# A banded convolution on TensorE quadrants: lag of the upper rows, order of the first pair of batches, and place of the transforms

## The chip, the cores and the metric

The kernel runs on one core of a Trainium2 chip. A core has a matrix engine (TensorE, "PE" in the profile, with "PEld" for its weight loads), VectorE ("DVE"), ScalarE ("ACT"), GpSimd ("POOL", which here also issues most of the DMAs) and SyncE ("SP"). The engines run side by side. Each takes its own instructions in the order of the program and waits on semaphores for the others. The metric is the device time of one execution in microseconds (us).

## The reference

The input `x` has shape (8, 3264, 192): batch, sequence, channels. Two layers follow each other.

The first is a causal convolution along the sequence. Each of 8 heads (24 channels each) has 7 taps, a softmax over `weight`:

```
w = softmax(weight, axis=-1)
u[b,s,c] = sum_k w[h(c),k] * x[b, s-6+k, c]        (zeros before s = 0)
```

The second mixes the lowest 64 frequencies and then a dense layer:

```
X = rfft(u, axis=1)[:, :64]
Y = X[b,m,:] @ (w_r[m] + i*w_i[m])                 (64 complex 192x192 matrices)
v = u + irfft(Y)
out = v + max(v @ w_ch, 0)
```

## The kernel before

The batches go in four pairs `q` (2 batches each). A sequence of 3264 is cut into 13 blocks of 256. A block lies in SBUF as 128 partitions by two rows: partition `p` holds positions 2p and 2p+1 of the block, and the choice between the two is called `a`. So a pair has 26 tiles of 128 rows (`NT`), and all of `x` in bf16 is the tile `xall`.

The convolution runs in units of blocks. Pair 0 has units of 3, 5 and 5 blocks, each later pair a unit of 7 and one of 6: nine units, with indices k = 0 to 8. A unit has 16 steps: 8 heads, and for each the output rows a = 0 and a = 1. A step is a product of a banded 64x64 matrix (tile `shared`, called `band`) with `n` blocks of one head (48n columns; 336 for n = 7, 288 for 6, 240 for 5, 144 for 3). TensorE is split into four 64x64 quadrants. A step has four matmuls on the lower 64 rows and four on the upper 64 rows, and all eight add into one PSUM bank (`conv_pieces`, matmuls at L299). Two row halves must not write one bank at the same time, so `conv_step` (L305) runs the lower rows of step k together with the upper rows of step k-2, and before them puts a `turn`: a wait of TensorE's queue until the lower rows of step k-2 have ended. Each step takes the next bank of a ring of seven (`conv_bank`, L284). `xtrans` takes two banks of the same ring.

A bank is emptied by a copy that casts to bf16 and writes back into `xall`: VectorE for a = 0 (L326), ScalarE for a = 1 (L328). The output of a unit goes one block lower than its input stood, in the slots that the halo of both steps of a head still reads. So the two copies of a head are emitted after the upper rows of its a = 1 step, and both wait for those.

Between the steps stand other works, in an order written out by hand in the loop at L378:

- `dft` (L330, matmuls at L334): the product of a finished tile of `xall` with 128 columns of cosines and sines (`ftab`), 26 tiles added up per pair in one bank of its own, which `xs` (L337) copies out. `dfts` issues them in groups: 3 and 3 in the second unit, 5 and 5 in the next two, up to 7 and 7 later, at heads 3 and 7 (5 and 7 in the second unit).
- `xtrans` (L339): 12 small matmuls that turn the frequencies of a pair for the mixing, with one copy on VectorE (L355) and one on ScalarE (L357); at head 1 of units 4, 6 and 8.
- `table` (L220): the cosine and sine table, in three parts of tiles and six operations each, three on VectorE (L224, L227, L229) and three on ScalarE (L231, L233, L235), spread by `extra` over the heads of the first three units.

Ahead of the loop VectorE computes the softmax and sets the taps in a packed band (seven `copy_predicated` for each half of the heads, L205). Four copies of 32 partitions for each half then put it in place, two on VectorE (L215) and two on ScalarE (L213). A dummy sine (L191) makes ScalarE load its sine table early. It writes `wrec`, which the reciprocal of the softmax (L195) writes next. TensorE meanwhile runs `NIDLE` = 28 matmuls on zeros.

GpSimd issues the loads of `x` (`load_unit`, L144), each casting from f32 in HBM. Between them it builds constants: `ident`, `perm`, `apart`, and parts of `wm` and `w1`. Then come the loads of the mixing matrices.

After the convolution follow the mixing by frequency (L458) among transposes (L419), from 80 to 119 us, and the inverse transform with the dense layer (L667, copies at L570 and L583), from 119 us to the end. The change does not touch them.

Of the kernel before, what the change touches and what calls it, by code (L numbers as in the profile page):

```python
# [10 lines left out]
ACT = mybir.ActivationFunctionType  # L11
AX = mybir.AxisListType
F32 = mybir.dt.float32
# [6 lines left out]
def kernel(  # L20
# [9 lines left out]
    nc = tc.nc  # L30
    B, S, D = x.shape
    H, KK = weight.shape
# [4 lines left out]
    P = 128  # L37
# [6 lines left out]
    BW = P + 2  # L44
    TWOPI = 6.283185
    MAGIC = 12582912.0
    NIDLE = 28
    UNITS0 = ((0, 3), (3, 5), (8, 5))
    UNITS = ((0, 7), (7, 6))
    units = [(q, b0, n) for q in range(NQ) for b0, n in (UNITS if q else UNITS0)]  # L50
# [3 lines left out]
    def sb(name, shape, dtype):  # L54
        return pool.tile([P] + shape, dtype, tag=name, name=name)
# [14 lines left out]
    band = shared[:, 0:H * 2 * BW].rearrange("p (h o c) -> p h o c", h=H, o=2)  # L70
# [7 lines left out]
    ascale = sb("ascale", [1], F32)  # L78
# [21 lines left out]
    def temp(n, dtype):  # L100
        w = n * 2 if dtype == F32 else n
        a = arena[:, pos[0]:pos[0] + w]
        pos[0] += (w + 15) // 16 * 16
        return a.bitcast(dtype) if dtype != BF16 else a
# [8 lines left out]
    wmax = temp(H, F32)  # L113
    wsum = temp(H, F32)
    wrec = temp(H, F32)
    cidx = temp(PW, F32)
    goff = temp(1, F32)
    masks = temp((KK // 2 + 1) * PW, U16)
# [25 lines left out]
    def load_unit(q, b0, n):  # L144
        nf = min(n, NB - 1 - b0)
        s0 = NB * q + b0 + 1
        for i in range(2):
            off = ((2 * q + i) * S + 2 * P * b0) * D
            src = bass.AP(tensor=x.tensor, offset=x.offset + off, ap=[[2 * D, P], [2 * P * D, nf], [1, 2 * D]])
            nc.gpsimd.dma_start(out=xin[:, s0:s0 + nf, 2 * D * i:2 * D * (i + 1)], in_=src)  # L150
        if nf < n:
            off = (2 * q * S + 2 * P * (NB - 1)) * D
            src = bass.AP(tensor=x.tensor, offset=x.offset + off, ap=[[2 * D, PL], [S * D, 2], [1, 2 * D]])
            nc.gpsimd.dma_start(out=xin[0:PL, s0 + nf, :].rearrange("p (i c) -> p i c", i=2), in_=src)
# [24 lines left out]
    zeros = xall[:, 0, 0, 0:P]  # L179
    for _ in range(NIDLE):  # L180
        nc.tensor.matmul(ZC[6], zeros, zeros.unsqueeze(1).to_broadcast([P, 4, P]), start=True, stop=True,
                         skip_group_check=True)
# [5 lines left out]
    nc.vector.tensor_tensor(out=wsub.rearrange("p (h k) -> p h k", h=H), in0=wr3,  # L188
                            in1=wmax.unsqueeze(2).to_broadcast([P, H, KK]), op=ALU.subtract)
    nc.scalar.activation(out=wexp, in_=wsub, func=ACT.Exp)  # L190
    nc.scalar.activation(out=wrec, in_=ascale.to_broadcast([P, H]), func=ACT.Sin)  # L191
    we3 = wexp.rearrange("p (h k) -> p h k", h=H)
    nc.vector.reduce_sum(out=wsum, in_=we3, axis=AX.X)
    nc.vector.tensor_scalar(out=wsum, in0=wsum, scalar1=1e-9, scalar2=None, op0=ALU.add)
# [6 lines left out]
    for h0 in (0, H // 2):  # L201
        hs = slice(h0, h0 + H // 2)
        for lag in range(KK):
            k = lag // 2
            nc.vector.copy_predicated(  # L205
                out=pk4[:, hs, lag % 2, :],
                mask=masks[:, PW * k:PW * (k + 1)].unsqueeze(1).to_broadcast([P, H // 2, PW]),
                data=ta3[:, hs, KK - 1 - lag:KK - lag].to_broadcast([P, H // 2, PW]))
        for g in range(4):
            c0 = 1 + 32 * (g % 2)  # L210
            dst, srcv = band[32 * g:32 * g + 32, hs, :, c0:c0 + PW], pk4[32 * g:32 * g + 32, hs, :, :]
            if g % 2:
                nc.scalar.copy(out=dst, in_=srcv)  # L213
            else:
                nc.vector.tensor_copy(out=dst, in_=srcv)  # L215
# [4 lines left out]
    def table(step, t0, t1):  # L220
# [13 lines left out]
        else:  # L234
            nc.scalar.activation(out=ftab[:, t0:t1, 0:2 * MODES - 1:2], in_=wh, func=ACT.Sin, scale=-TWOPI,  # L235
                                 bias=halfpi[:, 0:1])

    nc.gpsimd.memset(ident[:], 0.0)
    nc.gpsimd.affine_select(out=ident[:], in_=ident[:], compare_op=ALU.not_equal, fill=1.0,
                            base=0, pattern=[[-1, P]], channel_multiplier=1)  # L240
# [2 lines left out]
                            base=-64, pattern=[[-1, 64]], channel_multiplier=1)  # L243
    nc.gpsimd.affine_select(out=perm[:, 64:128], in_=perm[:, 64:128], compare_op=ALU.not_equal, fill=1.0,
                            base=0, pattern=[[-1, 64]], channel_multiplier=1)
    load_unit(*units[3])

    for i in range(2):
        nc.gpsimd.memset(apart[i][:], 0.0)
        for c in range(2):  # L250
# [6 lines left out]
                            fill=1.0, base=0, pattern=[[-1, D]], channel_multiplier=1)  # L257
    nc.gpsimd.affine_select(out=w1[64:P, D:2 * D], in_=w1[64:P, D:2 * D], compare_op=ALU.not_equal,
                            fill=1.0, base=P, pattern=[[-1, D]], channel_multiplier=1)
    for k, u in enumerate(units[4:]):  # L260
        load_unit(*u)
        if k == 1:
            nc.gpsimd.dma_start(out=wm[:, 0:D], in_=moe_w_ch[0:P, :])
        if k == 2:
            nc.gpsimd.dma_start(out=w1[64:P, 0:D], in_=moe_w_ch[P:D, :])
# [11 lines left out]
    def turn(names):  # L277
        nop = nc.tensor.nop()
        for name in names:
            tc.add_manual_dep(nop.ins, name, mybir.DependencyInfo(mybir.DependencyClass.Sync,  # L280
                                                                  mybir.DependencyReason.DATA),
                              reason="row tiles take turns on a bank")

    def conv_bank():  # L284
        npass[0] += 1
        return ZC[(npass[0] - 1) % 7]
# [14 lines left out]
                                       tile_position=(64 * row, 64 * col), skip_group_check=True).ins.name  # L301

    flow = []

    def conv_step(u):  # L305

        lower = upper = iter(())
        flow.append(None)
        if u is not None:
            flow[-1] = [(u, conv_bank()), []]  # L310
            lower = conv_pieces(flow[-1][0], 0)
        old = flow[-3] if len(flow) > 2 else None
        if old is not None:
            turn(old[1][2:])
            upper = conv_pieces(old[0], 1)
        for _ in range(4):
            if u is not None:
                flow[-1][1].append(next(lower))
            next(upper, None)
        if old is not None and old[0][0][4] == 1:  # L320
            for (q, b0, n, h, a), z in (flow[-4][0], old[0]):
                s0 = NT * q + 2 * b0 + a
                dst = xall[:, s0:s0 + 2 * n - 1:2, :, GRP * h:GRP * h + GRP]
                srcv = z[:, 0:2 * GRP * n].rearrange("p (b i e) -> p b i e", b=n, i=2)
                if a == 0:
                    nc.vector.tensor_copy(out=dst, in_=srcv)  # L326
                else:
                    nc.scalar.copy(out=dst, in_=srcv)  # L328

    def dft(q, t0, t1):  # L330
        xp = zf
# [7 lines left out]
    def xtrans(q, banks=None):  # L339
        if banks is None:  # L340
            banks = [conv_bank(), conv_bank()]
        for i in range(2):
            tp = banks[i][:, 0:3 * P].rearrange("p (j c) -> p j c", j=3)
            xsv = xs[q % 2][:, i, :].rearrange("k (p j) -> k j p", j=3)
            for j in range(3):
                nc.tensor.matmul(tp[0:64, j, :], xsv[:, j, :], apart[0][:], start=True, stop=True,  # L346
                                 tile_position=(0, 0), skip_group_check=True)
                nc.tensor.matmul(tp[64:P, j, :], xsv[:, j, :], apart[1][:], start=True, stop=True,
                                 tile_position=(0, 64), skip_group_check=True)
        for i in range(2):  # L350
            b = 2 * q + i
            dst = xt[:, :, b:2 * B:B, 0:MODES]
            srcv = banks[i][:, 0:3 * P].rearrange("p (j c m) -> p j c m", j=3, c=2)
            if i == 0:
                nc.vector.tensor_copy(out=dst, in_=srcv)  # L355
            else:
                nc.scalar.copy(out=dst, in_=srcv)  # L357

    p1, p2, p3 = (0, 6), (6, 16), (16, NT)
    extra = {(0, 1): ((0, *p1),), (0, 2): ((1, *p1),), (0, 3): ((2, *p1),), (0, 4): ((3, *p1),), (0, 5): ((4, *p1),),  # L360
             (0, 6): ((5, *p1), (0, *p2)), (1, 0): ((1, *p2),), (1, 2): ((2, *p2),), (1, 3): ((3, *p2),),
             (1, 4): ((0, *p3),), (1, 5): ((4, *p2),), (1, 6): ((1, *p3),), (1, 7): ((5, *p2),),
             (2, 0): ((2, *p3),), (2, 2): ((3, *p3),), (2, 4): ((4, *p3),), (2, 6): ((5, *p3),)}
    todo = []
    pend = []

    def dfts(n):
        while n > 0 and todo:
            q, t0, t1 = todo.pop(0)
            m = min(n, t1 - t0)  # L370
            dft(q, t0, t0 + m)
            n -= m
            if t0 + m < t1:
                todo.insert(0, (q, t0 + m, t1))
            elif t1 == NT:
                pend.append(q)

    for k, u in enumerate(units):  # L378
        for h in range(H):
            for a in range(2):  # L380
                conv_step((*u, h, a))
            for e in extra.get((k, h), ()):
                table(*e)
            if h == 1 and pend:
                xtrans(pend.pop(0))
            if k == 1 and h in (5, 7):
                dfts(3)
            elif k > 1 and h in (3, 7):
                dfts(5 if k < 4 else 7)
        if k == 3:  # L390
            for g in range(NW + 3):
                load_w(g)
        todo.append((u[0], 2 * u[1], 2 * (u[1] + u[2])))
    for _ in range(2):
        conv_step(None)
    dfts(99)
    nc.gpsimd.memset(yet[:, :, 2 * B * (MODES - 8):2 * B * MODES], 0.0)
    zt4 = open_psum("left", (1, 1, 1, 1))
# [357 lines left out]
```

## Time and profile before

| | |
|---|---|
| median of three runs | 184.71 us (184.31 to 184.81) |
| the profiled execution's own time | 184.13 us |
| its span, first to last instruction | 182.3 us |
| TensorE busy | 167.5 us, 92% of the span |
| VectorE busy | 129.2 us, 71% |
| ScalarE busy | 113.8 us, 62% |
| GpSimd busy | 52.2 us, 29% |
| chain that ended last | TensorE 83%, VectorE 9%, ScalarE 3% |
| copies of the convolution on VectorE (L326) | 72 of 448 ns in the mean |
| copies of the convolution on ScalarE (L328) | 72 of 388 ns in the mean |
| transform matmuls (L334) | 104 of 327 ns |

The span leaves out 1.8 us of the execution's own time. A line of the timeline gives the start in us, the time in us, the engine, the line of the kernel, the operation, out<-in, the number of instructions that the line merges, and in brackets how long the engine had been idle and what ended that. Two forms of a group differ in shape, so a mean over a whole line mixes units of different size. A matmul's time reaches from its start to the end of its pipeline, so matmuls overlap.

### The profile page before, as it was taken

Reading aid. Unit: us, or ns where it says so; the run is one execution under the profiler, and the core shown is the slowest. Engines: PE = TensorE matmul, PEld = TensorE weight load, DVE = VectorE, ACT = ScalarE, POOL = GpSimd, SP = SyncE. Lnnn points to the kernel's source line nnn. Section 1 sums busy time; section 2 is a strip of 40 time slices with the busy share of each in tenths; the row PEclk is TensorE's granted clock in tenths of the full one; section 3 lists DMA queues with packets and bytes.
Section 4 is the critical chain, followed back from the end, with each engine's and each line's share of the span. In section 5 each row is a group of like instructions: output and inputs, shape, how many; then the busy total and the mean of one; then the engine's idle time right before and its main releaser. Section 6 shows DMA issues by size and latency. Waiting matters only on the chain.

```text
span 182.3 us, 7178 instructions
## 1 busy us (share of the span) xinstructions
PE 167.5 (92%) x2970; PEld 123.9 (68%) x2970; DVE 129.2 (71%) x278; ACT 113.8 (62%) x239; POOL 52.2 (29%) x95
## 2 busy tenths in 40 slices
PE   6949999999999999879999998899999999999990
PEld 2437554555555565458999946479989999999960
DVE  6698865555555464346877813679899999999992
ACT  5356866554564364238777724468888888888870
POOL 7997332334224442026503400088000000000000
PEclk9996999999999999999999999999999999999999
DMA  3999999999999999929995992058999898989996
GB/s 48 149 198 203 207 201 203 205 206 199 204 204 207 206 207 206 201 51 160 198 207 94 162 191 39 0 168 305 351 323 347 319 363 316 366 332 341 351 343 229
DMA packets 37392, 40.15 MB, mean 220 GB/s; under 512 B 2512, under 2 KB 37360, under 8 KB 37360
## 3 DMA queue, kind: packets, MB, share of 16 engines
q0 software_dynamic: 22848, 19.62, 68.4%
q1 hardware_dynamic: 14512, 20.09, 30.1%
q8 instruction: 23, 0.38, 0.8%
q14 instruction: 9, 0.07, 0.1%
HBM read 39.10 MB, written 20.05 MB: 324 GB/s over the span
## 4 chain that ended last, share of the span: by engine, by line
PE 83%; DVE 9%; ACT 3%; issue 2%; DVEq 0%; ACTq 0%
PE z L667 32%; PE z L299 21%; PE z L419 11%; PE z L334 10%; PE z L458 3%; DVE xall L326 2%; DVE arena L205 2%; PE z L537 1%; PE z L346 1%; PE z L594 1%; PE z L605 1%; PE z L528 1%; DVE xall L175 1%; PE z L538 1%; ACT L191 1%
## 5 line engine op out<-in xcount | busy, mean ns | idle before, releaser
L570 DVE TENSOR_TENSOR arena<-z,xall 128x384 f32<-128x384 f32 (+1 forms) x104 | 57.0, 556 | 3.3 <-PE z L667 1.3
L583 ACT ACTIVATE z<-z 128x384 f32<-128x384 f32 x102 | 48.5, 475 | 12.1 <-PE z L667 2.4
L326 DVE CAST xall<-z 128x336 bf16<-128x336 f32 (+3 forms) x72 | 32.0, 448 | 25.5 <-PE z L299 22.3
L299 PE MATMUL z<-xall,shared 64*64 64x288 bf16 (+3 forms) x1152 | 44.1, 290 | 4.9 <-DVE xall L326 3.8
L667 PE MATMUL z<-arena,ftab 64*128 64x384 bf16 x308 | 44.9, 322 | 0.0
L667 PEld LDWEIGHTS <-ct 64*128 64x128 bf16 x600 | 42.3, 94 | 3.7 <-PE z L594 0.6
L328 ACT CAST xall<-z 128x336 bf16<-128x336 f32 (+3 forms) x72 | 27.6, 388 | 24.5 <-PE z L299 21.3
L299 PEld LDWEIGHTS <-shared 64*64 64x64 bf16 x1152 | 27.4, 108 | 21.5 <-issue 9.4
L667 PE MATMUL z<-wsw,ct 64*128 64x192 bf16 x300 | 35.1, 243 | 0.0
L667 PEld LDWEIGHTS <-ftab 64*128 64x128 bf16 x396 | 29.7, 93 | 2.7 <-issue 0.5
L667 PE MATMUL z<-wm,ct 64*128 64x192 bf16 x200 | 29.9, 243 | 0.0
L667 PE MATMUL z<-w,ct 64*128 64x192 bf16 x100 | 24.3, 243 | 0.0
L411 DVE COPY ct<-z 128x1024 bf16<-128x1024 bf16 x26 | 17.1, 687 | 5.1 <-PE z L419 3.6
L334 PE MATMUL z<-xall,ftab 128*128 128x384 bf16 (+1 forms) x104 | 19.8, 327 | 0.6 <-DVE xall L326 0.6
L419 PE MATMUL z<-ident,xall 128*128 128x128 bf16 x312 | 19.3, 219 | 0.2 <-ACT ftab L409 0.2
L150 POOL DMA_DIRECT2D xall<-in_x_dram x18 | 15.8, 879 | 12.3 <-DMA xall<-in_x_dram 11.4
L419 PEld LDWEIGHTS <-xall 128*128 128x128 bf16 x312 | 17.7, 98 | 1.0 <-issue 0.3
L272 POOL DMA_DIRECT2D arena<-in_moe_w_r_dram x13 | 8.1, 622 | 32.0 <-PE z L458 24.2
L409 ACT COPY ct<-z 128x1024 bf16<-128x1024 bf16 x13 | 13.2, 1012 | 4.2 <-PE z L419 4.0
L334 PEld LDWEIGHTS <-ftab 128*128 128x128 bf16 (+1 forms) x104 | 8.9, 98 | 9.0 <-issue 4.5
L667 PE MATMUL z<-mixa,ftab 64*128 64x384 bf16 x88 | 13.6, 323 | 0.0
L485 POOL DMA_DIRECT2D arena<-xs x16 | 7.9, 504 | 14.7 <-ACT xs L481 14.6
(108 smaller groups left out, 135.7 us busy)
## 6 DMA issues: line engine op xcount, KB each, us to landing
out_dram<-arena SPq DMA_DIRECT2D x47, 384.0 KB, 3.5
xall<-in_x_dram POOLq DMA_DIRECT2D x6, 672.0 KB, 16.1
xall<-in_x_dram POOLq DMA_DIRECT2D x8, 480.0 KB, 15.7
arena<-in_moe_w_r_dram POOLq DMA_DIRECT2D x13, 288.0 KB, 8.2
arena<-in_moe_w_i_dram POOLq DMA_DIRECT2D x13, 288.0 KB, 9.0
ct<-in_moe_w_r_dram POOLq DMA_DIRECT2D x3, 288.0 KB, 11.7
ct<-in_moe_w_i_dram POOLq DMA_DIRECT2D x3, 288.0 KB, 11.7
out_dram<-arena SPq DMA_DIRECT2D x3, 288.0 KB, 3.0
```

Source lines behind the costliest of these rows:

```text
L150: nc.gpsimd.dma_start(out=xin[:, s0:s0 + nf, 2 * D * i:2 * D * (i + 1)], in_=src)
L272: nc.gpsimd.dma_start(out=wts[g][64 * half:64 * half + 64, :, :, :], in_=src[4 * g:4 * g + 4, :, :].rearrange("m (p j) e -> p m j e", j=3))
L299: yield nc.tensor.matmul(o, band[r, h, int(a != a1), c0:c0 + 64], xin5[r, s1:s1 + n, :, a1, dsl], start=(row == 0 and a1 == 0), stop=(row ...
L326: nc.vector.tensor_copy(out=dst, in_=srcv)
L328: nc.scalar.copy(out=dst, in_=srcv)
L334: nc.tensor.matmul(xp, ftab[0:k, t, :], xall[0:k, NT * q + t, :, :], start=(t == 0), stop=(t == NT - 1), skip_group_check=True)
L409: nc.scalar.copy(out=out, in_=in_)
L411: nc.vector.tensor_copy(out=out, in_=in_)
L419: nc.tensor.matmul(o, in_, ident[:], start=True, stop=True, is_transpose=True)
L570: nc.vector.tensor_tensor(out=o[0:pn, :, a, :], in0=bank[0:pn, 0:2 * D].rearrange("p (i d) -> p i d", i=2), in1=xall[0:pn, s + a, :, :], o ...
L583: nc.scalar.activation(out=z, in_=z, func=ACT.Relu)
L667: mm = nc.tensor.matmul(target(bank[k], cols, r), l, r, start=first, stop=last, skip_group_check=True)
```

## The change

- The upper rows run three steps behind the lower ones instead of two (`CONVLAG` = 3). `conv_step` takes the old step and the pair to copy one place further back.
- The copies of the two rows change engines: a = 0 goes to ScalarE, a = 1 to VectorE.
- Pair 0 runs unit by unit: after each of its three units a new `flush` issues the upper rows that are still open (three calls without a new step) and empties the list. Then come all transforms of that unit, and after the third unit also `xtrans` of pair 0. After the first unit's flush, six matmuls of 512 columns on the band run ahead of the transforms.
- From unit 4 on the transforms come once per unit, all 12 or 14 tiles at head 2, after the `xtrans` if one is open. In unit 3 there are none.
- The table's operations have other places in the first three units: up to three at one head.
- All four band copies of the first half of the heads are on ScalarE, all four of the second half on VectorE.
- The dummy sine writes a tile of its own, `wsin`.
- `NIDLE` is 27. The loads of units 3 and 4 are issued ahead of the constants on GpSimd; the loads of `wm` and `w1` come one unit later.

```diff
-    NIDLE = 28
+    NIDLE = 27
...
-    nc.scalar.activation(out=wrec, in_=ascale.to_broadcast([P, H]), func=ACT.Sin)
+    nc.scalar.activation(out=wsin, in_=ascale.to_broadcast([P, H]), func=ACT.Sin)
...
-            if g % 2:
+            if h0 == 0:
                 nc.scalar.copy(out=dst, in_=srcv)
             else:
                 nc.vector.tensor_copy(out=dst, in_=srcv)
...
+    load_unit(*units[3])
+    load_unit(*units[4])
     nc.gpsimd.memset(ident[:], 0.0)
...
-    load_unit(*units[3])
...
-    for k, u in enumerate(units[4:]):
+    for k, u in enumerate(units[5:]):
...
+    CONVLAG = 3
...
-        old = flow[-3] if len(flow) > 2 else None
+        old = flow[-1 - CONVLAG] if len(flow) > CONVLAG else None
...
-            for (q, b0, n, h, a), z in (flow[-4][0], old[0]):
+            for (q, b0, n, h, a), z in (flow[-2 - CONVLAG][0], old[0]):
...
                 if a == 0:
+                    nc.scalar.copy(out=dst, in_=srcv)
+                else:
                     nc.vector.tensor_copy(out=dst, in_=srcv)
-                else:
-                    nc.scalar.copy(out=dst, in_=srcv)
+
+    def flush():
+        for _ in range(CONVLAG):
+            conv_step(None)
+        flow.clear()
...
-    extra = {(0, 1): ((0, *p1),), (0, 2): ((1, *p1),), (0, 3): ((2, *p1),), (0, 4): ((3, *p1),), (0, 5): ((4, *p1),),
-             (0, 6): ((5, *p1), (0, *p2)), (1, 0): ((1, *p2),), (1, 2): ((2, *p2),), (1, 3): ((3, *p2),),
-             (1, 4): ((0, *p3),), (1, 5): ((4, *p2),), (1, 6): ((1, *p3),), (1, 7): ((5, *p2),),
-             (2, 0): ((2, *p3),), (2, 2): ((3, *p3),), (2, 4): ((4, *p3),), (2, 6): ((5, *p3),)}
+    extra = {(0, 0): ((0, *p1), (1, *p1), (2, *p1)), (0, 3): ((3, *p1), (4, *p1)), (0, 5): ((5, *p1),),
+             (0, 7): ((0, *p2), (1, *p2), (2, *p2)), (1, 1): ((3, *p2),), (1, 2): ((4, *p2), (0, *p3)),
+             (1, 3): ((5, *p2),), (1, 4): ((1, *p3),), (1, 6): ((2, *p3),), (1, 7): ((3, *p3),),
+             (2, 1): ((4, *p3),), (2, 3): ((5, *p3),)}
...
-            if h == 1 and pend:
-                xtrans(pend.pop(0))
-            if k == 1 and h in (5, 7):
-                dfts(3)
-            elif k > 1 and h in (3, 7):
-                dfts(5 if k < 4 else 7)
+            if k > 3 and h == 2:
+                if pend:
+                    xtrans(pend.pop(0))
+                dfts(99)
...
-    for _ in range(2):
-        conv_step(None)
+        if u[0] == 0:
+
+            flush()
+            if k == 0:
+                z = conv_bank()
+                for _ in range(6):
+                    nc.tensor.matmul(z, band[:, 0, 0, 0:P], band[:, 0, 0:1, 0:P].to_broadcast([P, 4, P]), start=True, stop=True,
+                                     skip_group_check=True)
+            dfts(99)
+            if pend:
+                xtrans(pend.pop(0))
+    flush()
     dfts(99)
```

More of the change, by code (lines that the diff above doesn't have):

```diff
@@ L115 @@
     wrec = temp(H, F32)
+    wsin = temp(H, F32)
     cidx = temp(PW, F32)
```

## The prediction

> **What bounds the kernel now.** I read the stages by window first, then who waited for whom, then the timeline, and last the groups by shape. The stage that changes ends with the last transform at 78.05 us; what follows only moves with it.
>
> ```profile
> 9.90:15.40 5.50, 3.32 (x109) 2.62 (x112) 5.09 (x19) 2.83 (x9) 5.29 (x13) 0.93 1.30 201
> 15.40:18.20 2.80, 2.80 (x72) 2.17 (x68) 2.37 (x6) 2.13 (x8) 1.75 (x3) 0.54 1.31 203
> 18.20:28.90 10.70, 10.00 (x228) 5.76 (x224) 7.76 (x19) 8.51 (x19) 3.67 (x5) 1.00 1.32 204
> 51.30:66.50 15.20, 14.87 (x299) 8.64 (x302) 8.17 (x17) 7.65 (x18) 6.11 (x10) 1.00 1.24 206
> ```
>
> Columns: stretch, length, busy time of PE, PEld, DVE, ACT and POOL, granted clock, DMA share and rate. From 51.3 TensorE has work for 14.87 of 15.20 us, VectorE for half. In units 1 and 2 (18.2 to 28.9) ScalarE is busy 80%: the tables run there.
>
> ```profile
> PE z L299 <- DVE xall L326: 3.8, 8, 1.6
> ```
>
> TensorE waits for a copy to free a bank, never for a load of `x`. Why there:
>
> ```profile
> 69.47 0.44 PE L299 MATMUL z<-xall,shared 64*64 64x288 bf16 x8 [0.33 <-DVE xall L326]
> 69.84 0.93 PEld L334 LDWEIGHTS <-ftab 128*128 128x128 bf16 x7 [0.22 <-issue]
> 69.84 1.31 PE L334 MATMUL z<-xall,ftab 128*128 128x384 bf16 x7
> 69.98 0.40 ACT L328 CAST xall<-z 128x288 bf16<-128x288 f32 x1 [0.63 <-PE z L299]
> 70.05 0.46 DVE L326 CAST xall<-z 128x288 bf16<-128x288 f32 x1 [0.64 <-PE z L299]
> ...
> 74.54 0.68 PE L299 MATMUL z<-xall,shared 64*64 64x288 bf16 x8
> ...
> 75.27 0.40 ACT L328 CAST xall<-z 128x288 bf16<-128x288 f32 x1 [1.42 <-PE z L299]
> 75.33 0.46 DVE L326 CAST xall<-z 128x288 bf16<-128x288 f32 x1 [1.36 <-PE z L299]
> 75.85 0.97 PE L334 MATMUL z<-xall,ftab 128*128 128x384 bf16 x5 [0.62 <-DVE xall L326]
> ```
>
> One step (n = 6) lasts 0.44 us from first start to last end. Both copies of a head start after the a = 1 step has ended, ScalarE 0.07 and VectorE 0.14 us later. TensorE resumes 0.05 us after a copy. At 74.54 the last two half steps take almost the time of two full ones, then 0.62 us pass before the transform.
>
> ```profile
> L326 DVE CAST xall<-z 128x336 bf16<-128x336 f32 x24 | 12.2, 507 | 9.3 <-PE z L299 8.0
> L328 ACT CAST xall<-z 128x336 bf16<-128x336 f32 x24 | 10.5, 439 | 8.1 <-PE z L299 6.5 <-DVE xall L326 0.3
> L328 ACT CAST xall<-z 128x240 bf16<-128x240 f32 x16 | 5.5, 357 | 2.9 <-PE z L299 2.0 <-DVE arena L227 0.5
> ```
>
> ```profile
> 25.98 2.08 PE L299 MATMUL z<-xall,shared 64*64 64x240 bf16 x64
> ```
>
> Eight steps of n = 5 take 2.08 us, the last of them 0.40: (2.08 - 0.40)/7 = 0.24 us a step. The same rows give 0.29 for n = 7 (2.51 for eight, the last 0.48) and 0.25 for n = 6 (1.45 for five).
>
> **The change, part by part.**
>
> *Lag of three, copies swapped.* Step s uses bank s mod 7. Its copy waits for the upper rows of the a = 1 step. With lag 2, an a = 0 bank on VectorE comes free 0.48 + 0.14 + 0.51 + 0.05 = 1.18 us after step s+3 starts (n = 7), and step s+7 needs it: four steps of 0.29 = 1.16. The kernel sits just at this limit. With lag 3 the upper rows of that a = 1 step run in step s+4, so ScalarE frees the bank 0.48 + 0.08 + 0.44 + 0.05 = 1.05 us after s+4 starts, and only three steps, 0.87, lie between: 0.18 us of stall in every four steps. For n = 6 it is 0.44 + 0.07 + 0.40 + 0.05 = 0.96 against 0.75, so 0.21; for n = 5 it is 0.88 against 0.72. The a = 1 bank (VectorE, 1.18 after s+3) has four steps and fits.
> A unit of 16 steps pays four times, one of them hidden by the transforms in its middle. Unit 3 (no transforms) pays 0.72, unit 4 0.63, units 5 and 7 0.54 each. In units 6 and 8 `xtrans` takes two banks, so five steps, not seven, lie between uses. Steps 7 and 9 each need a bank whose copy waits for the step just before: 0.96 - 0.25 = 0.71 twice. With 0.17 at the second bank of `xtrans`, 0.3 before it and 0.2 after, that is 2.1 each. Sum: 6.6 us. The turn that the lag loosens never shows in the list of waits; at most a step of n = 5 falls to two passes of 240 columns at the transform's pace (0.161 us for 384), 0.20: 0.04 x 32 = 1.3 us, lost behind the banks. I take 0.
>
> *Transforms once per unit.* The chain charges 1.24 us for a group of seven and 0.92 for five, 0.16 a matmul plus 0.12, and the eight steps ahead of a group 2.45 instead of 8 x 0.29 = 2.32: about 0.24 us a group. 17 groups become 9: -1.9. The three stalls like that at 69.47 (three steps from 68.19 on would have put it at 68.95, so 0.51 late) go: -1.5; those at steps 7 and 9, counted above, are next.
>
> *Pair 0 unit by unit.* I follow each queue.
> Start: without the dummy sine's write the reciprocal goes at 6.05, not 7.11 (a wait of 1.09 us). Seven predicated copies end at 8.3 and four ScalarE band copies of 0.44 at 10.1; the first steps start after two of these, 9.3 against 9.90. VectorE places its band copies by 11.1, then, ahead of any copy of a bank, three table operations (0.57 + 0.35 + 0.54) until 13.0. Step 8 needs a VectorE copy: 13.1, where before step 7 waited until 13.01. ScalarE's Sin and Abs (1.16) delay step 11 to 14.3. Step 15 runs at 15.6, the half steps end near 16.6. But VectorE has three table operations (0.82 + 0.48 + 0.82) ahead of its last two copies: these end at 18.1. The six warming matmuls at the half clock (0.54 in the second row above) end by 18.6. Six transforms, 1.1 us: unit 1 starts at 19.7.
> Unit 1: ScalarE's first copy starts at 19.7 + 4 x 0.24 + 0.47 = 21.1. Two copies of 0.36 and table operations of 0.75 and 1.02 run before the copy that step 11 needs: 24.0 instead of 22.3. Eight more steps: 25.9. The last Sin (0.92) stands ahead of ScalarE's last two copies, behind VectorE's operation that ends at 25.4: 27.2. Ten transforms, 1.7: unit 2 at 29.0 to 29.5; I take 29.3.
> Unit 2, in the same way with one Sin of 1.02: step 11 at 32.9, half steps done at 34.8, copies at 35.5, transforms at 37.2, `xs` 0.48, `xtrans` 0.5: unit 3 at 38.4.
> Before, unit 3 starts at 28.9 with ten transforms (2.1) and `xtrans` with its stall (1.2) left, so 32.2. **Pair 0 costs 6.2 us.** If the table operations hid wholly it would be about 1 (flushes 9 half steps x 0.24 and three waits of 0.6, against 3.3 us of merging and unhindered band).
>
> *Units 3 to 8.* 48 steps x 0.29 + 48 x 0.25 = 25.9; 66 transforms x 0.161 + 5 x 0.24 = 11.8; two `xtrans` 1.1; stalls 6.6: 45.4. Three half steps 0.75 and the last copy 0.84: the last transforms start at 38.4 + 47.0 = 85.4 against 75.85. **+9.5 us.**
>
> *At nothing.* One idle matmul less: TensorE then waits for the band anyway (0.73 us); else -0.3. The earlier issue of units 3 and 4: DMA share and 200 GB/s are already full, and TensorE waited for no load. GpSimd's constants slip from 7.4-13.8 to about 15-19.5, behind loads that wait for landings (11.4 us in all), and may slow the second tables: ±0.4, from a 26-element operation at 0.65 us beside them against 0.18 for one like it. Their first use is the `xtrans` at 38. The mixing matrices follow `x` on the same full queue.
>
> The profiled time was 184.13, 182.3 of it span: 193.6. The median is 0.58 above that profile: **194.2 us**.
>
> **The rivals.**
> *A, banks come free in time*, so that the pace stays as it is: 6.6 less, and up to 2 less in units 1 and 2: 185.6 to 187.6. For it: a copy takes 0.51 of a pair of 0.58 us, so no engine is full. Against: the copies stand behind the a = 1 step in every row above. The Trainium skill, TensorEngine Tiling, PSUM Bottleneck, says that the copies may bound a tiled product, and advises to use both engines. By that throughput alone this rival would come out, 0.51 being below 0.58; the row at 69.47 shows a stall of latency, not of throughput.
> *B, faster.* The turn, not the bank, paces the steps. Then lag 3 brings 1.3 (n = 5), some 0.9 for the rest, 1.9 of merging and 1.5 of `xtrans`: 5.6. It decides only if pair 0 costs below that, so with tables hidden: 1 - 5.6 gives 180.1, half hidden 183. Against: no wait for a turn beyond one of 0.26 us.
> *C, the clock falls again.* Before, it was halved for 3.4 us after a stretch with 3.32 busy of 5.50 us and no gap over 1.6. Units 1 and 2 have waits of about 1 us several times. One more halving there doubles about eight steps of 0.24: +2, so 196.2, two 198. The Trainium skill, TensorE: Matmul & The Clock Gate, HAM oscillation, says that gaps over some 3.4 us bring the halved clock. By that none would come; the trace had one without such a gap.
>
> **How the numbers follow.** Forecast 0.63 (own range 191.5 to 196), C 0.17, A 0.13, B 0.04, equal within 0.3% (about what a measurement can tell from no change) 0.03. Range 187.0 to 198.0: forecast, C and half of A. Faster 0.04, same 0.03, slower 0.93.
>
> **What would show it.** Right: PE L299 waits for ACT copies every fourth step, twice about 0.7 us after each `xtrans`; unit 3 starts near 38; the last transforms near 85; VectorE's last copies of unit 0 stand behind L224 to L229. Wrong: eight steps of n = 7 in unit 5 in 2.5 us, or unit 3 before 34.

## The result and the profile after

The changed kernel takes 192.83 us (192.73 to 193.44, four runs), the kernel before beside it 184.51 us (184.29 to 184.81). The ratio is 1.0457, with a 95% interval of 1.0428 to 1.0485: 8.3 us slower. Forecast were 194.2 us and +9.5.

The profiled execution took 192.88 us, with a span of 191.1 us. The stages by window, after (stretch, length, busy time of PE, PEld, DVE, ACT and POOL, granted clock, DMA share and rate):

```profile
9.90:15.40 5.50, 3.57 (x115) 2.70 (x114) 4.19 (x13) 2.80 (x9) 2.33 (x6) 0.89 1.28 197
15.40:18.20 2.80, 2.80 (x29) 1.60 (x26) 2.56 (x6) 0.90 (x4) 2.59 (x9) 0.60 1.31 204
19.50:28.30 8.80, 6.62 (x141) 4.87 (x142) 4.58 (x11) 5.35 (x12) 4.79 (x7) 1.00 1.32 204
49.30:65.90 16.60, 15.45 (x302) 10.53 (x298) 8.25 (x17) 7.64 (x18) 6.49 (x11) 1.00 1.25 205
```

The last row is units 5 and 6, one n = 7 and one n = 6. Before, one unit of each kind took 15.2 us with TensorE idle for 0.33; now it is 16.6 with 1.15 idle. VectorE and ScalarE do the same work as before, so what grew is waiting.

Who TensorE waits for after 28 us, after the change, in the list of waits:

```profile
PE z L301 <- ACT xall L329: 2.6, 5, 0.5
PE z L342 <- ACT xall L329: 0.9, 2, 0.5
```

The copies it waits for are now ScalarE's (L329), where before it was VectorE's. This list misses most of it, since a busy matmul reaches to the end of its pipeline and so covers a short wait. The timeline shows them by the rhythm of the copies. Unit 5 (n = 7) behind its transforms, and unit 6 behind `xtrans`, after:

```profile
53.55 4.96 PE L301 MATMUL z<-xall,shared 64*64 64x336 bf16 x120
...
54.10 1.01 ACT L329 CAST xall<-z 128x336 bf16<-128x336 f32 x2
...
55.43 1.01 ACT L329 CAST xall<-z 128x336 bf16<-128x336 f32 x2 [0.32 <-PE z L301]
...
56.76 1.01 ACT L329 CAST xall<-z 128x336 bf16<-128x336 f32 x2 [0.32 <-PE z L301]
```

```profile
61.81 0.44 PE L301 MATMUL z<-xall,shared 64*64 64x288 bf16 x8
62.32 0.40 ACT L329 CAST xall<-z 128x288 bf16<-128x288 f32 x1 [2.31 <-PE z L301]
...
62.77 0.68 PE L301 MATMUL z<-xall,shared 64*64 64x288 bf16 x16 [0.53 <-ACT xall L329]
63.53 0.40 ACT L329 CAST xall<-z 128x288 bf16<-128x288 f32 x1 [0.81 <-PE z L301]
...
63.98 1.18 PE L301 MATMUL z<-xall,shared 64*64 64x288 bf16 x32 [0.52 <-ACT xall L329]
```

In the first, two copies of ScalarE stand for four steps, and they come every 1.33 us. Four steps of 0.285 would be 1.14, so 0.19 is lost each time (0.18 forecast). In the second, a step at 61.81 is followed by one at 62.77, 0.96 later, and the next pair again waits, from 63.02 to 63.98: 0.72 lost twice (0.71 forecast).

Pair 0, the end of unit 1, after:

```profile
24.27 0.82 DVE L230 TENSOR_TENSOR arena<-arena 128x640 f32<-128x640 f32 x1
25.01 1.03 DVE L331 CAST xall<-z 128x240 bf16<-128x240 f32 x3
25.13 0.92 ACT L232 ACTIVATE ftab<-arena 128x640 bf16<-128x640 f32 x1 [0.47 <-DVE arena L230]
25.91 0.59 ACT L329 CAST xall<-z 128x240 bf16<-128x240 f32 x2
26.55 1.78 PE L342 MATMUL z<-xall,ftab 128*128 128x384 bf16 x10 [1.24 <-ACT xall L329]
```

VectorE's table operation holds ScalarE's Sin, and that holds the last two copies. The transforms start 0.05 us behind them, and TensorE is idle for 1.24 us. Unit 3 starts at 36.87 us (the start of a unit is that of its first matmul in the trace), the last transforms at 83.94 (before 75.85). So 8.1 of the 8.8 us by which the two profiled spans differ are there by the end of the convolution. The mixing starts at 88.29 instead of 80.20, also 8.1 later.

### The profile page after: what moved, and what is told of

It is laid out like the page before. It is cut to its first block, busy times and chain, and to the rows that moved or that the text cites. A ratio compares the mean times of both kernels' runs of the same rounds, so it can differ in the third digit from the quotient of the medians.

```text
span 191.1 us, 7179 instructions
## 1 busy us (share of the span) xinstructions
PE 172.6 (90%) x2975; PEld 135.2 (71%) x2975; DVE 130.3 (68%) x278; ACT 114.1 (60%) x239; POOL 52.8 (28%) x95
## 4 chain that ended last, share of the span: by engine, by line
PE 80%; DVE 7%; ACT 7%; issue 3%; DVEq 0%; ACTq 0%
PE z L683 31%; PE z L301 20%; PE z L435 11%; PE z L342 9%; ACT xall L329 3%; PE z L474 3%; DVE arena L206 2%; PE z L553 1%; PE z L354 1%; PE z L406 1%; PE z L610 1%; PE z L621 1%; PE z L544 1%; DVE xall L176 1%; PE z L554 1%
## 5 line engine op out<-in xcount | busy, mean ns | idle before, releaser
L301 PE MATMUL z<-xall,shared 64*64 64x336 bf16 (+3 forms) x1152 | 46.1, 286 | 5.9 <-ACT xall L329 3.8
L301 PEld LDWEIGHTS <-shared 64*64 64x64 bf16 x1152 | 35.1, 109 | 17.1 <-issue 14.9
L683 PE MATMUL z<-arena,ftab 64*128 64x384 bf16 x308 | 45.4, 322 | 0.0
L329 ACT CAST xall<-z 128x336 bf16<-128x336 f32 (+3 forms) x72 | 27.6, 390 | 27.0 <-PE z L301 23.5
L683 PE MATMUL z<-wsw,ct 64*128 64x192 bf16 x300 | 39.9, 243 | 0.0
L683 PE MATMUL z<-wm,ct 64*128 64x192 bf16 x200 | 32.8, 243 | 0.0
L683 PEld LDWEIGHTS <-ftab 64*128 64x128 bf16 x396 | 27.6, 93 | 1.9 <-issue 0.7
L342 PE MATMUL z<-xall,ftab 128*128 128x384 bf16 (+1 forms) x104 | 18.5, 326 | 2.2 <-ACT xall L329 2.2
L274 POOL DMA_DIRECT2D arena<-in_moe_w_r_dram x13 | 8.1, 622 | 38.4 <-PE z L474 33.6
L342 PEld LDWEIGHTS <-ftab 128*128 128x128 bf16 (+1 forms) x104 | 9.7, 97 | 9.5 <-issue 3.6
```

Source lines behind the costliest of these rows:

```text
L274: nc.gpsimd.dma_start(out=wts[g][64 * half:64 * half + 64, :, :, :], in_=src[4 * g:4 * g + 4, :, :].rearrange("m (p j) e -> p m j e", j=3))
L301: yield nc.tensor.matmul(o, band[r, h, int(a != a1), c0:c0 + 64], xin5[r, s1:s1 + n, :, a1, dsl], start=(row == 0 and a1 == 0), stop=(row ...
L342: nc.tensor.matmul(xp, ftab[0:k, t, :], xall[0:k, NT * q + t, :, :], start=(t == 0), stop=(t == NT - 1), skip_group_check=True)
L683: mm = nc.tensor.matmul(target(bank[k], cols, r), l, r, start=first, stop=last, skip_group_check=True)
```

## The experiments

Two theories, one for each half of the loss. **Banks**: with a lag of three the a = 0 bank is needed three steps, not four, after the upper rows of the a = 1 step begin, and a copy does not get done in that. **Queues**: in pair 0 table operations stand ahead of the last copies, and the drains wait for them. The rivals put the loss on the drains alone, on the turn, or on the engines of the copies. Each kernel was timed beside the kernel before on one chip.

### The lag alone, undone and done

```diff
-    CONVLAG = 3
+    CONVLAG = 2
```

> The changed kernel with a lag of two steps instead of three, all else as changed. Bank theory (the copies of a head wait for the upper rows of its a = 1 step, and with a lag of three only three steps are left until the a = 0 bank is needed): the waits every fourth step go (four steps of 0.29 = 1.16 us hold the 1.05 that ScalarE needs), the two waits of 0.71 after each xtrans shrink; 5.5 us less than the changed kernel: 187.3 (186.5 to 188.2). Rival one, the whole loss is in pair 0 (drains and refills) and the lag costs nothing: 192 to 193, less three half steps (0.6). Rival two, the turn paces the steps: slower than 193.

187.47 us (187.16 to 187.95), 1.0166 of before (1.0138 to 1.0194): 5.4 us less than the change. In the two profiles the gain lies behind pair 0: unit 3 starts only 0.14 us earlier (36.73), and from there to the last transforms it is 42.3 us instead of 47.1. The other way round, on the kernel before:

```diff
-        old = flow[-3] if len(flow) > 2 else None
+        old = flow[-4] if len(flow) > 3 else None
...
-            for (q, b0, n, h, a), z in (flow[-4][0], old[0]):
+            for (q, b0, n, h, a), z in (flow[-5][0], old[0]):
...
-    for _ in range(2):
+    for _ in range(3):
```

> The kernel before with a lag of three steps as its only change, so VectorE keeps the copies of a = 0. Bank theory: an a = 0 bank is free 0.48 + 0.14 + 0.51 + 0.05 = 1.18 us after step s+4 (n = 7) and needed three steps (0.87) later: 0.31 every four steps, 0.34 for n = 6, more after each xtrans; in all about +10 us: 194.5 (192.5 to 197). Rival, the lag alone costs nothing and all of the loss is the order of pair 0: 184 to 186.

195.21 us (194.74 to 195.91), 1.0595 (1.0561 to 1.0629): +10.9. Units 5 and 6 take 18.25 us (from 48.71 to 66.96, first matmul of unit 5 to first of unit 7), 15.18 before (44.18 to 59.36). Eight steps, in its timeline:

```profile
48.71 3.07 PE L299 MATMUL z<-xall,shared 64*64 64x336 bf16 x64
...
50.69 1.01 ACT L328 CAST xall<-z 128x336 bf16<-128x336 f32 x2 [0.45 <-PE z L299]
50.74 1.09 DVE L326 CAST xall<-z 128x336 bf16<-128x336 f32 x2 [0.38 <-PE z L299]
```

Eight steps take 3.07 us where they took 2.51 before, in this row:

```profile
44.18 2.51 PE L299 MATMUL z<-xall,shared 64*64 64x336 bf16 x64
```

Both results lie where the bank theory put them. A lag that costs nothing is out.

### The copies' engines, and shorter copies

```diff
                 if a == 0:
-                    nc.vector.tensor_copy(out=dst, in_=srcv)
-                else:
                     nc.scalar.copy(out=dst, in_=srcv)
+                else:
+                    nc.vector.tensor_copy(out=dst, in_=srcv)
```

> The kernel before with the copies of a = 0 on ScalarE and of a = 1 on VectorE as its only change. Bank theory: the bank that is needed first then comes free after 1.05 instead of 1.18 us and the kernel leaves the limit of four steps (1.16): 0.3 to 1.2 us faster, 183.8 (183.3 to 184.2). Rival, the engines are not what limits and the swap is nothing: 184.5; if VectorE's slower copy of the late row hurts: 185 or more.

183.26 us (182.86 to 183.63), 0.9944 (0.9925 to 0.9963): 1.1 us faster. Units 5 and 6 take 14.83 us instead of 15.18. In this profile the clock was not halved around 16 us, as it was before, but that is not the gain: unit 3 starts only 0.13 us earlier (28.78 against 28.91), the rest comes behind it. So the swap in the change is a gain by itself, and a step of the loss it is not.

```diff
-                dst = xall[:, s0:s0 + 2 * n - 1:2, :, GRP * h:GRP * h + GRP]
-                srcv = z[:, 0:2 * GRP * n].rearrange("p (b i e) -> p b i e", b=n, i=2)
+                dst = xall[:, s0:s0 + 1, :, GRP * h:GRP * h + GRP]
+                srcv = z[:, 0:2 * GRP].rearrange("p (b i e) -> p b i e", b=1, i=2)
```

> The changed kernel with copies that empty only the first block of each bank (48 columns); the other blocks of xall keep x as loaded, so that part of the convolution's output is left out. Nothing else moves. Bank theory: a copy of about 0.20 us frees the bank after 0.48 + 0.08 + 0.20 + 0.05 = 0.81 us, less than three steps of n = 7 (0.87) and just three of n = 6 (0.76 against 0.75): the waits every fourth step vanish and those after xtrans fall from 0.71 to 0.5; with shorter queues in units 1 and 2 it is 6 to 7 us less than the changed kernel: 186.4 (185.3 to 187.5). Rival, the lag costs nothing and pair 0's drains are the loss: only the three waits at the ends of its units shorten, 0.6 to 1.5 us less: 191.3 to 192.2.

187.15 us (186.59 to 187.30), 1.0149 (1.0124 to 1.0174): 5.7 us less than the change, a little short of the number and inside its range. The copies took 198 ns on ScalarE and 207 on VectorE. The lag was still three and the drains were still there. Some 1.7 us of the gain are pair 0's shorter queues (unit 3 starts at 35.15 instead of 36.87). Behind that units 5 and 6 take 14.85 us instead of 16.60, so the banks' part rests on the length of a copy, as it should. It doesn't tell latency from an overloaded engine by itself; the windows do, with each engine busy for half of the stage.

### Pair 0

On the kernel before, with a lag of two, pair 0 as in the change (the diff is that part of the change's own):

> The kernel before with pair 0 unit by unit as in the change (flush, here of two steps, six warming matmuls, all transforms of the unit, xtrans after the third) and the change's places of the table operations; lag of two, copies, start and later units as before. Queue theory (table operations stand ahead of the last copies on VectorE and ScalarE, so that the drain at a unit's end waits for them): 5.5 us more than before: 189.9 (188.7 to 191.2). Rival, only the drain and refill cost: six half steps of 0.24 and three waits of 0.6 less three merged groups (0.7): +2.5, 186.9.

191.04 us (190.91 to 191.52), 1.0367 (1.0347 to 1.0387): +6.6, inside the range and far from the rival. The nearness to the forecast is in part chance: unit 1 starts at 22.07 us, in the change at 19.49, because of a long wait and a halved clock (both below) that the theory did not have. Then the table operations for tiles 6 to 25 taken out:

```diff
+    nc.gpsimd.memset(ftab[:, 6:NT, :], 0.0)
...
             for e in extra.get((k, h), ()):
-                table(*e)
+                if e[1] == 0:
+                    table(*e)
```

> The same with the table operations for tiles 6 to 25 left out (those columns of the table are zeros that GpSimd sets once, so the transforms of these tiles give nothing); the operations of tiles 0 to 5 stay. Queue theory: the copies are no longer behind them, 3.5 to 4.5 us less than the kernel with the tables: 185.9 (185.0 to 187.0). Rival, the drains alone are the cost and the tables are hidden: no change by more than 1 us, 189 to 190.

189.82 us (188.84 to 190.10), 1.0286 (1.0248 to 1.0323): only 1.2 us less, 3.9 above what I expected and outside the range. In the profiles unit 3 starts 2.5 us earlier than with the tables (36.11 against 38.58), 1.9 of it won in units 1 and 2; why the end keeps only 1.2 is not shown. In unit 0 two things stood in the way of more. The first shows in TensorE's timeline of this kernel:

```profile
18.07 2.53 PE L406 MATMUL z<-shared 128*128 128x512 bf16 x6
20.44 1.14 PE L340 MATMUL z<-xall,ftab 128*128 128x384 bf16 x6
```

VectorE's last copy of unit 0 ended at 18.56 us, but the six warming matmuls ran until 20.6 at half the clock: they had taken the place of the tables as what the transforms wait for. Second, with the old start the three table operations at the first head hold the first copies longer than in the change: step 7 waits 3.1 us here and 3.4 in the kernel with the tables. After that the clock was halved for 6.8 us in both, twice the time of the change. The windows of the kernel with the tables:

```profile
10.00:14.50 4.50, 1.45 (x48) 1.03 (x48) 4.22 (x14) 1.58 (x5) 4.29 (x12) 1.00 1.30 199
14.50:21.40 6.90, 6.46 (x89) 3.63 (x89) 4.36 (x12) 2.82 (x9) 4.43 (x6) 0.51 1.31 203
```

So I put the same two questions again within the change, with a lag of two (187.47 us). First pair 0 as before: the flush, the warming and the transforms behind them out, the old `extra`, and in the loop

```diff
+            elif k == 1 and h in (5, 7):
+                dfts(3)
+            elif k in (2, 3) and h in (3, 7):
+                dfts(5)
```

> The changed kernel with a lag of two and with pair 0 as it was before: no flush, no warming matmuls, transforms in groups of 3 and 5 among the steps, the table operations at their old places; xtrans of pair 0 at head 2 of unit 4. Start, copies and transforms once per unit from unit 4 on stay as changed. Theory: everything that is left of the change is a gain, so 181.2 (180.3 to 182.3), and the unit by unit order of pair 0 costs about 6 us of the 187.5 that the lag of two leaves. Rival, pair 0's order costs only the 3.1 us by which the lag of two stands above the kernel before: 184.4.

180.54 us (180.24 to 180.80), 0.9787 (0.9761 to 0.9813). The unit by unit order costs 6.9 us. Then the tables, as in the diff above:

> The changed kernel with a lag of two and without the table operations for tiles 6 to 25 (zeros set once by GpSimd, so that those transforms give nothing); flush, warming matmuls and all else stay. Queue theory: units 1 and 2 lose their waits behind ScalarE's table operations (about 1.8 and 0.7 us), unit 0 gains nothing because the warming matmuls end only when VectorE's last copies did: 185.0 (184.2 to 185.9). Rival, drains and warming matmuls are all of pair 0's cost: 187 or more.

183.59 us (182.39 to 184.59), 0.9950 (0.9921 to 0.9979): 3.9 us less than with the tables, more than I gave the queues and just outside the range; the runs of this kernel scatter by 2.2 us. In the traces the step from unit 1 to unit 2 shrinks from 9.17 to 6.47 us, from unit 2 to unit 3 from 8.41 to 7.58, and unit 1 starts no earlier (19.44 against 19.15). So of 6.9 us some 3.9 are copies behind tables, taking it that the tables cost nothing at their old places, which no run shows. The other 3.0 are the drains, the half-filled steps, the warming matmuls, a serial `xtrans` and the clock, which in the profiles was halved for 3.4 us near 17 us with the order of the change, and not with the old one. I did not separate these.

### The start, the grouping, and what is left when the good parts are kept

```diff
-    NIDLE = 28
+    NIDLE = 27
...
-    nc.scalar.activation(out=wrec, in_=ascale.to_broadcast([P, H]), func=ACT.Sin)
+    nc.scalar.activation(out=wsin, in_=ascale.to_broadcast([P, H]), func=ACT.Sin)
...
-            if g % 2:
+            if h0 == 0:
```

> The kernel before with the change's start only: dummy sine into its own tile, band copies of the first half of the heads all on ScalarE and of the second all on VectorE, 27 idle matmuls; loads as before. Theory: the predicated copies begin 1.06 us earlier and VectorE reaches its first copy of a bank about 1 us sooner (in the change itself three table operations stand there, so that it gained nothing): 183.5 (183.0 to 184.2). Rival, the start is hidden or the four copies in a row on ScalarE eat it: 184.3.

183.97 us (183.31 to 184.59), 0.9970 (0.9953 to 0.9987): 0.5 us faster, half of what I expected. In the profile step 7 starts at 11.80 instead of 13.01, and the clock stays full from 15.4 to 18.2 (1.00 where it was 0.54). Unit 3 starts at 27.58 instead of 28.91, 1.3 earlier; the last full step at 73.72 instead of 74.54, 0.8 earlier, and this 0.8 is still there in the mixing at 113 us. At the end the two spans are equal (182.3): in the last 17 us of this profile the granted clock was 0.94, before 1.00. I did not follow why. So the gain of the start is real where it arises, and parts of it are given back in two later places. How much of it is the fuller clock's is not shown.

> The kernel before with the transforms of units 4 to 8 once per unit at head 2, behind the xtrans, as in the change; lag of two, pair 0 and copies as before. Theory: five groups fewer at 0.24 us, 1.2 less, and the stall after xtrans (0.51, three times) partly stays since xtrans takes two banks of the ring: 183.3 (182.6 to 184.0). Rival, 14 transforms in a row starve the copies' engines and the steps before them wait, nothing gained: 184.3 or more.

The edit is the loop of the change from unit 4 on, with the groups of 3 and 5 kept before. 183.14 us (182.89 to 183.34), 0.9933 (0.9916 to 0.9950): 1.35 us faster, as expected.

Last, the parts that gain, on the kernel before: the swap, a lag of two, and

```diff
             if h == 1 and pend:
                 xtrans(pend.pop(0))
             if k == 1 and h in (5, 7):
                 dfts(3)
-            elif k > 1 and h in (3, 7):
-                dfts(5 if k < 4 else 7)
+            elif k in (2, 3) and h in (3, 7):
+                dfts(5)
+            elif k > 3 and h == 2:
+                dfts(99)
```

> What is of use put together on the kernel before: lag of two, copies of a = 0 on ScalarE and of a = 1 on VectorE, transforms of units 4 to 8 once per unit at head 2, but xtrans one head earlier, at head 1 as before, so that the two steps between them run on free banks and the copies after them fall beside the transforms. Pair 0 and the start as before. Bank theory: no wait every fourth step, five groups of 0.24 saved, the three stalls of 0.51 after xtrans gone: 0.9 + 1.2 + 1.5 = 3.6 less, 180.8 (180.0 to 181.8). Rival, grouping and swap do not add up: 182.5 to 183.3.

181.16 us (180.79 to 181.29), 0.9820 (0.9807 to 0.9834). With the start of the change as well:

> The same with the change's start as well (sine into its own tile, band copies half by half, 27 idle matmuls): 0.8 less than without, 180.0 (179.2 to 181.3). Rival, the clock or the tables take it back: no difference.

179.73 us (179.61 to 180.12), 0.9748 (0.9734 to 0.9761): 4.7 us faster than the kernel before and 13.1 faster than the change. The start is worth 1.4 us here, where alone it brought 0.5. The new order of the loads was not tried alone; the kernel that has it, with `xtrans` at head 2 (180.54 us above), is 0.8 us slower than this one, so the two together cost no more than about that. One pair of units in its windows, and a unit's copies in its timeline:

```profile
9.90:15.40 5.50, 3.84 (x136) 2.90 (x139) 5.41 (x16) 2.76 (x10) 5.29 (x13) 1.00 1.30 199
15.40:18.20 2.80, 2.65 (x87) 1.84 (x83) 2.44 (x7) 1.83 (x7) 2.23 (x4) 1.00 1.30 197
48.50:62.50 14.00, 14.00 (x306) 8.28 (x299) 8.15 (x18) 7.67 (x19) 4.39 (x9) 1.00 1.26 206
```

```profile
45.62 3.63 PE L300 MATMUL z<-xall,shared 64*64 64x336 bf16 x96
...
46.46 2.72 ACT L327 CAST xall<-z 128x336 bf16<-128x336 f32 x5 [0.26 <-PE z L300]
```

Two units take 14.0 us with TensorE busy in all of it. Five copies of ScalarE follow every two steps (2.72 us, 0.57 apart), where in the change they came in twos with a pause. Behind `xtrans` at head 1 no stall shows: the two steps after it take 0.69 us (from 50.16), the transforms follow at 50.77, and the copies catch up meanwhile.

## Why the prediction was right

The time lay 1.4 us below the forecast, and in its range. In the sum the lag stood for 6.6 us of loss and pair 0 for 6.2, the transforms once per unit for 3.4 of gain (1.9 and 1.5). Undone one after the other, the lag gave back 5.4 and the order of pair 0 6.9, and what was left of the change was 3.7 us faster than the kernel before (180.54 against 184.28 us). The borders differ a little (the swap stood in the 6.6, the new start in the 6.2), but no part was off by more than about 1.5 us. By its own steps:

- **Lag of three.** Forecast stalls of 0.18 (n = 7) and 0.21 (n = 6) in every four steps, and 0.71 twice after `xtrans`; the trace has 0.19, 0.22 to 0.23 and 0.72. Units 3 to 8 up to the last transforms were worked out at 47.0 us and took 47.1 (36.87 to 83.94); unit by unit, the terms are off by 0.23 us at most. The part that the lag has in this, 5.4 us by the undoing, was 6.6 in the sum; a lag of two keeps some of the stall after `xtrans`, which takes two banks either way.
- **The swap** I had only as part of the stall's length; it is worth 1.1 us alone.
- **Transforms once per unit**: 0.24 us a group held. Five groups (1.2 us) brought 1.35, and unit 5, with one group less and no `xtrans`, took 6.84 us instead of 7.06.
- **The turn.** I took 0 for what a looser turn brings, with 0.20 a step of n = 5 at most. Behind a lag of three those steps do run at 0.205 us (20.03 to 20.65 in unit 1, three steps), against 0.235 before. Nearly all of it was lost behind banks and tables, as put; 0.13 us shows in unit 1 (next point).
- **Pair 0** is the term that was too large: 6.2 us up to unit 3's start at 38.4. It was 4.7, the start lying at 36.87. (The new start's gain is in both numbers, so they are not the 6.9 of the experiment.) Unit 1 took 8.8 us instead of 9.6, unit 2 8.6 instead of 9.1. Step 11 of unit 1 came 0.8 us earlier than worked out (23.20 against 24.0), for three reasons. The unit began 0.2 earlier. ScalarE's first copy then came after 1.30 us instead of 1.43 (at 20.79 against 21.1), since I had used 0.24 us for the steps instead of the 0.20 that I had myself named as the floor. The largest part, 0.46, lies in ScalarE's queue. There I had added whole durations, but each operation starts 0.10 to 0.15 us before the end of the one ahead of it:

```profile
20.79 0.36 ACT L329 CAST xall<-z 128x240 bf16<-128x240 f32 x1 [1.74 <-PE z L301]
21.05 0.74 ACT L234 ACTIVATE arena<-arena 128x640 f32<-128x640 f32 x1
21.69 0.35 ACT L329 CAST xall<-z 128x240 bf16<-128x240 f32 x1
21.93 1.02 ACT L236 ACTIVATE ftab<-arena,halfpi 128x640 bf16<-128x640 f32 x1
22.80 0.61 ACT L329 CAST xall<-z 128x240 bf16<-128x240 f32 x2
```

And unit 2 was put at 29.3 where the terms give 27.2 + 1.7 = 28.9; no term stood for the 0.4 between. The statement that pair 0 would cost about 1 us with hidden tables is not borne out: 3.0 are left with the tables of tiles 6 to 25 out, though the halved clock and the tables of tiles 0 to 5 are still in these.

- **At nothing**: TensorE did not wait for the band after the idle matmuls. They ran until 10.46 us, because in that execution the clock was full only from 7.4 us on (their weight loads come every 0.43 us up to 7.1, and 12 of them in 2.47 us behind that), and the first step, put at 9.3, followed at once at 10.38. The cover was gone, and it cost nothing only since step 8 waits for VectorE's copy until 13.30 (13.1 forecast).
- **Rival C**, a further halving of the clock, did not happen in the change (one stretch of 3.4 us, 0.60 in 15.4 to 18.2, as before). Its mechanism showed in the kernel with pair 0 alone, at 0.51 for 6.9 us. Rivals A and B fell with the two kernels on the lag.

## What to carry to other kernels

A ring of buffers has a budget in steps: bring the wait of each copy to its true last reader, count the steps from there to the next use, and set it against pipeline end, semaphore, copy and wake-up. An added step of lag takes from that budget what it gives to another wait, and here 0.2 to 0.3 us of missing budget in every four steps, and more behind `xtrans`, were 5 to 11 us. Where a pipeline is drained, look at what else stands in the queues of the engines that finish it: work that was hidden beside full steps is on the path there.

## What the runs showed of the hardware that I had not expected

The clock was halved after stretches in which TensorE had gaps, most of them short. In the changed kernel it was busy for 3.57 of 5.50 us with no gap over 1.4, and the clock fell for 3.4 us; with 3.84 of 5.50 busy and no gap over 0.5, in the last kernel, it stayed full, and so it did in the kernel with the new start alone (3.89 busy, no gap over 0.7). After a wait of 3.4 us with 1.45 of 4.50 busy it fell for 6.8 us. The Trainium skill, TensorE: Matmul & The Clock Gate, HAM oscillation, speaks of gaps over some 3.4 us: only the last of these fits that, the others fell with shorter ones.

The busy time of those 5.5 us and the longest gap do not decide it either. In the kernel before with the transforms once per unit, TensorE was busy for 4.13 of 5.50 us with no gap over 1.0, and the clock fell:

```profile
9.90:15.40 5.50, 4.13 (x113) 2.90 (x113) 5.17 (x19) 2.83 (x9) 5.29 (x13) 0.88 1.29 196
15.40:18.20 2.80, 2.80 (x76) 2.06 (x69) 2.37 (x6) 2.17 (x9) 2.17 (x4) 0.63 1.31 203
```

Between its first and last change the clock keeps a value for 3.41 us or a multiple of it in every trace here. So the stretch to look at is the 3.41 us that end where the clock falls. In the convolution TensorE worked 1.55 us of these in the changed kernel, 1.39 in the kernel before, 2.04 in the kernel just shown, and no more in any other that fell. The full clock came back after 3.41 us with 3.15 or more of work, and not after 3.02 (pair 0 alone) or 1.96 (the same with the tables out), which therefore stayed halved for 6.8. A sharp limit is not shown: 1.93 us of work with a gap of 1.3 (a lag of two with the old pair 0, from 14.98 on) and 2.02 (a lag of two, from 25.21 on) were followed by the full clock.

In the kernel with pair 0 alone and the tables out, the six 512-column matmuls that were to keep the clock up took 2.53 us, 0.42 each, and were themselves what the transforms waited for.
